# Reordering steps 19 to 50 and the casts beside 128-token tiles in a fused attention, MLP and expert kernel

## The chip, the cores and the metric

One core of a Trainium2 chip runs the whole kernel. The metric is device time in microseconds, the median of several runs; lower is better. TensorE's two clock levels are 1.2 and 2.4 GHz; the profile gives the granted share of the upper one.

## The reference, cut to what matters

Attention with keys and values averaged over groups of 8, then a dense ELU layer, then a top-1 mixture of 8 experts:

```python
k_p = k.reshape(B, H, Sp, 8, D).mean(axis=3)        # B=8, H=8, S=576, Sp=72, D=64
v_p = v.reshape(B, H, Sp, 8, D).mean(axis=3)
attn = softmax(q @ k_p.T / 8)                        # 576 x 72 per head
x = concat_heads(attn @ v_p)                         # 4608 tokens x 512
h = x @ w_in                                         # 512 -> 2048, w_in as float64
x = elu(h) @ w_out                                   # 2048 -> 512, w_out as float64
e = argmax(x @ w_gate); p = softmax(x @ w_gate)[e]   # 8 experts
out = p * (relu(x @ w1[e]) @ w2[e])                  # 512 -> 1024 -> 512
```

## The kernel before, in words

Work is put on the engines by hand: within a stretch, the order in which Python calls the helpers is the order of each engine's own queue.

**The dense layer** has 12 blocks of 384 tokens (3 tiles of 128) and 16 slices of the hidden width, so 192 steps. Step n does `g1_mm` (12 matmuls into one of two `h` banks of PSUM), the ELU, and `g2` of step n-2 (9 matmuls into the three `y` banks). An operand is split in a high and a low half (`xh`, `xl`; `gh`, `gl`). On ScalarE (ACT) a step has `elu_a` (three activations, lines 517 to 519) and the cast `gh` (line 531); on VectorE (DVE) `elu_b` (lines 524 and 525) and `gl` (line 532). Because there are two `h` banks, `h` of step n+2 waits until `elu_b` of step n has read its bank. When a block, or a quarter of blocks 0 and 1, ends, the three `y` banks are emptied (`y_rows`, lines 563 to 567, or `y_join`, line 589) before the next block's first `g2` may write them.

Other work is hung into named slots of a step through `at(n, slot, fn, ...)`; the order of the slots stands in `step`. Four kinds of it matter here.

- Steps 0 to 27 decode the float64 weights: `w_mul` (ACT, line 221), `w_bits` (DVE, lines 226 to 232), `w_hi` (ACT, line 243), `w_lo` (DVE, line 246). The later decode tiles, the parked partial sums that `y_fetch` brings back (SP queue, line 582) and nothing else by then share a ring of four buffers (tag `st`).
- Attention tiles 6 to 35: `s_mm` (32 small matmuls, line 411), `s_max` (DVE, line 418), `s_exp` (ACT, line 427, four heads a call), `s_norm` (DVE, lines 431 to 433). Up to tile 8, `t_mm` transposes on TensorE and `t_copy` empties the banks (line 471); from tile 9 on `q_turn` (DVE, line 447) and `q_move` (ACT and DVE by turns, line 455) do it in blocks. `pv_mm` (line 480) and `pv_copy` follow. Three banks (`bank_a`) serve `s_mm`, `t_mm` and `pv_mm`.
- Gate logits: `r_logit` (DVE, line 600), one for each expert and tile; `route_at` has a list of how many go into each step.
- `y_park` and `y_fetch` move partial sums of blocks 0 and 1 to memory and back.

**The experts** come as a list of tiles: D (512 tokens), S (256), T (128), U (32). `mix(n)` does a quarter n of them in turn: first matmuls `m_g1` (line 1249), second matmuls `m_g2` of the quarter before (line 1284), `m_act` (lines 1261 and 1262), `m_out` (lines 1301 and 1303), then the small U tile that runs beside it, then block moves of a later tile's rows (`m_move`, line 1155: 8 copies on ACT and 8 on DVE), then `ahead`. That is a planner: it loads weights (SP queue) and splits them into halves (`m_split`: casts on ACT, line 130, differences on DVE, line 131) up to a reach in estimated time and as far as slots of 4 KB are free. T tiles T0, T1 and T2 are quarters 28 to 31, 36 to 39 and 44 to 47; a T quarter has 16 first and 6 second matmuls. Tiles that are not "turned" by block moves (D0 to D3, T, U) are transposed on TensorE (line 1181), 88 transposes of 128x128 in all.

Of the kernel before, what the change touches and what calls it, by code (L numbers as in the profile page):

```python
# [10 lines left out]
F32 = mybir.dt.float32  # L11
# [87 lines left out]
def fused_kernel(ctx: ExitStack, tc: tile.TileContext, q, k, v, w_in, w_out, w_gate, w1, w2, cst, out):  # L99
# [459 lines left out]
    def y_rows(blk, plus=None):  # L559
        yr = mrpool.tile([P, TB, ROW], F32, tag="yr", name=f"yr{blk}")  # L560
        for j in range(TB):
            if plus:
                nc.vector.tensor_add(yr[:, j, :DM], plus[j], ys[blk][j])  # L563
            elif j % 2 == 0:
                nc.scalar.copy(yr[:, j, :DM], ys[blk][j])  # L565
            else:
                nc.vector.tensor_copy(yr[:, j, :DM], ys[blk][j])
        return yr
# [128 lines left out]

    SCORE0 = (6, 8)

    def score_at(t, n, slot="pe_mid"):  # L700
        at(n, slot, s_mm, t)
        n += slot == "pe_end"
        for hh in range(2):
            at(n, "dve_pre", s_max, t, hh)
        at(n, "act_mid", s_exp, t, 0)
        n += t not in (7, 8)
        at(n, "act_mid", s_exp, t, 1)
        at(n, "dve_mid" if t in SCORE0 else "end", s_norm, t)

    def turn_at(t, n):  # L710
        at(n + 1, "end", q_turn, t)
        for part in range(2):
            at(n + 2 + part, "act_mid", q_move, t, part)

    def trans_at(t, n):
        at(n, "pe_end" if t in OUT else "pe_mid", t_mm, t)
# [15 lines left out]
    for t in range(2 * TB, NT):  # L732
        if t not in SCORE:
            blk, j = divmod(t, TB)
            SCORE[t] = (NF * (blk - 1) + 5 * j - 2 if blk > 3 else 2 * NF - 1 + 5 * j, "pe_mid")
            if t > T_TURN:
                at(SCORE[t][0], "pe_mid", pv_mm, t - 1)
                at(SCORE[t][0], "act_mid", pv_copy, t - 1)
            at(SCORE[t][0] - 6, "end", a_load, t)
        else:  # L740
            at(SCORE[t][0] - 6, "end", a_load, t)
        score_at(t, *SCORE[t])
        if t >= T_TURN:
            turn_at(t, SCORE[t][0])
        else:
            trans_at(t, TRANS[t])
    at(NF * (NBLK - 1) - 2, "pe_mid", pv_mm, NT - 1)
# [53 lines left out]
    at(3 * QF + 1, "evac", y_park, 1, 1)  # L801
    at(5 * QF + 1, "evac", y_park, 0, 2, 0)
    for j in range(TB):
        at(4 * QF + 1 + j, "end", y_fetch, 0, j)
        at(6 * QF + 2 + j, "end", y_fetch, 1, j)
        at(7 * QF + 1 + j, "act_end", y_fetch, 2, j)

# [16 lines left out]
            at(n + 3, "pe_mid", r_count, blk)  # L824
            at(n + 3, "end", r_put, blk)

    route_at(1, 30, [1, 2, 2, 2, 2, 3, 3, 3, 3, 3])
    route_at(0, 41, [2, 2] + [3] * 6 + [2])
    route_at(2, 3 * NF + LAG + 1, [2, 2, 2, 2, 3, 3, 3, 3, 4])
    for blk in range(3, last):  # L830
        route_at(blk, NF * (blk + 1) + LAG, [3, 2, 3, 2, 3, 2, 3, 2, 2, 2])
# [306 lines left out]
    def m_turn(it, half):  # L1138
# [7 lines left out]
            nc.vector.transpose(t[:, x], g[:, x, :DM].rearrange("p (b f c) -> p b c f", b=4, c=KC))  # L1146
        spun[it, half] = t

    def m_move(it, half):
        name = f"{it[0]}{it[1]}_{half}"  # L1150
        t = spun.pop((it, half))
        w = moved[it, half] = w_tile([P, KC, 2, P], F32, f"zm{name}")
        for n, (a, b) in enumerate((a, b) for a in range(4) for b in range(4)):
            copy = (nc.vector.tensor_copy, nc.scalar.copy)[n % 2]
            copy(
                w[BL * b:BL * (b + 1), :, :, BL * a:BL * (a + 1)],
                t[BL * a:BL * (a + 1), :, b].rearrange("p x c t -> p c x t"),
            )
        w_free(f"zt{name}")

    def m_trans(it, u):
        kind, s = it
        if u == 0 and kind in "DS":
            zs[it, 0] = [pools[0].tile([P, KC, 2 * ST], F32R, tag=f"z{x}", bufs=1, name=f"z{x}{kind}{s}") for x in "hl"]
        if it in turned:
            half = {0: 0, turned[it]: 1}.get(u)
            if (it, half) in moved:
                src = moved.pop((it, half)).rearrange("p c x t -> p c (x t)")
                hi, lo = (z[:, :, 2 * P * half:2 * P * (half + 1)] for z in zs[it, 0])
                nc.scalar.copy(hi, src)  # L1170
                nc.vector.tensor_sub(lo, src, hi)
                w_free(f"zm{kind}{s}_{half}")
            return
        t = rows.pop((it, u))
        if u == 0:
            gates[it] = pools[0].tile([P, 4], F32, tag="gate", bufs=6, name=f"gate{kind}{s}")
        nc.vector.tensor_copy(gates[it][:, u:u + 1], t[:, DM:DM + 1])
        ps = bank_z([P, KC, P], f"zT{kind}{s}_{u}")
        t = t[:, :DM].rearrange("p (k c) -> p c k", c=KC)
        for c in range(KC):  # L1180
            nc.tensor.transpose(ps[:, c], t[:, c], ident)  # L1181
        if kind in "TU":
            z = mrpool.tile([P, KC, P], F32, tag="wgb1", name=f"zf{kind}{s}")
            nc.scalar.copy(z, ps)
            zs[it, 0] = z
            return
        hi, lo = (z[:, :, u * P:(u + 1) * P] for z in zs[it, 0])
        nc.scalar.copy(hi, ps)
        nc.vector.tensor_sub(lo, ps, hi)

    def m_load(it, i):
        kind, s = it
        regs, at = where[it]
        if i == 0:
            e = nc.sync.value_load(regs[0:1, 0, at:at + 1], min_val=0, max_val=NE - 1)
            wts[it] = [e]
        e = wts[it][0]
        if kind in "DS":
            st = staged(f"w1st{kind}{s}_{i}").rearrange("p (c f) -> p c f", c=KC)
        else:  # L1200
            st = w_tile([P, KC, 2 * P], F32, f"t1{kind}{s}_{i}")
        nc.sync.dma_start(
            st, w1[bass.ds(e, 1), :, 2 * P * i:2 * P * (i + 1)].rearrange("o (p c) f -> p (o c) f", p=P)
        )
        if kind == "U":
            st2 = w_tile([P, 2, DM], F32, f"t2{s}_{i}")
        else:
            st2 = staged(f"w2st{kind}{s}_{i}").rearrange("p (c d) -> p c d", c=2)
        nc.sync.dma_start(
            st2, w2[bass.ds(e, 1), 2 * P * i:2 * P * (i + 1), :].rearrange("o (c p) d -> p (o c) d", p=P)  # L1210
        )
        raws2[it, i] = st, st2
# [132 lines left out]
    def u_g2(it):  # L1345
# [4 lines left out]
        for n, (i, u) in enumerate(terms):  # L1350
            for j in range(4):
# [6 lines left out]
                    stop=n == len(terms) - 1,  # L1358
                )
        w_free(*(f"t{y}{k}{s}_{i}" for i in range(4) for y, k in (("1", "U"), ("2", ""))))  # L1360
        o = mrpool.tile([P, P], F32, tag="yr", name=f"uo{s}")
        nc.scalar.mul(o, ps, gates[it][:, 0:1])
        scatter(out.rearrange("n (j d) -> (n j) d", j=4), o, sidxs[it][0][:, 1:2], 4 * NTOK)
# [76 lines left out]
    for k in range(1, len(main)):  # L1440
        kind, prev = main[k][0], main[k - 1][0]
        for u in range(TILES[kind]):
# [4 lines left out]
            else:  # L1447
                n = 4 * k - 1
            (trans_late if prev != "T" and u > 1 else trans_at).setdefault(n, []).append((main[k], u))
    moves = {}  # L1450
    for k in range(TURN_FROM, len(main)):
        it, far = main[k], main[k - 1][0] == "T"
        if it[0] != "T":
            turned[it] = 1 + far
            n = 4 * k - 4 if far else 4 * k - 1
            if it[0] == "D":
                plan = ((3, m_turn, 0), (2, m_move, 0), (2, m_turn, 1), (1, m_move, 1))
# [40 lines left out]
    def mix(n):  # L1498
# [12 lines left out]
            m_out(main[k0], i0)  # L1511
        if k in side:
            (m_trans_side, u_g1, u_trans, u_g2)[i](side[k])
        for fn, it2, half in moves.pop(n, ()):
            fn(it2, half)
        ahead(n)
        for fn, *args in chores.pop(n, ()):
            fn(*args)
        if n == 13:
# [35 lines left out]
    def alone(it):  # L1555
# [9 lines left out]
        if it[0] == "U":  # L1565
            u_g1(it)
            u_trans(it)
            u_g2(it)
            return
        for i in range(4):  # L1570
            m_g1(it, i)
# [66 lines left out]
```

## Time and profile before

| | |
|---|---|
| median of 3 runs | 1367.85 us (1367.63 to 1370.15) |
| profiled execution | 1372.5 us, of which the span is 1370.4 us |
| TensorE busy | 98% of the span (weight loads 85%) |
| VectorE, ScalarE, GpSimd busy | 74%, 59%, 15% |
| mean granted clock | 0.994 |
| steps 0 to 191 of the dense layer | from 25.4 us to 918.9 us |

A row of the timeline gives start and length in us, engine, line, operation and tiles, and in brackets the idle time of the engine before it and what ended it. TensorE is nearly always busy, so the rows to look for are the few in which TensorE itself has such a bracket, and above them the row of the engine that is named there.

### The profile page before, as it was taken

How to read it: one execution, taken by the hardware profiler on the slowest of the kernel's cores; microseconds unless marked ns; L12 is line 12 of the kernel's file. 1: busy time of each engine (PE TensorE's matmuls, PEld its weight loads, DVE VectorE, ACT ScalarE, POOL GpSimd, SP SyncE). 2: the span in 40 equal slices, each digit the busy share in tenths (PEclk: the TensorE clock that was granted, in tenths of full speed). 3: DMA queues.
4: the chain of work that ended last, by engine and by line, in shares of the span. 5: the costliest groups of instructions: out<-in, count | busy, mean ns of one | idle time of the engine just before them, and what ended most of it. 6: DMA issues, size and time to landing. Idle time of an engine off the chain costs nothing.

```text
span 1370.4 us, 23752 instructions
## 1 busy us (share of the span) xinstructions
PE 1345.3 (98%) x8409; PEld 1159.5 (85%) x8410; DVE 1020.8 (74%) x2467; ACT 801.8 (59%) x1952; POOL 209.9 (15%) x208
## 2 busy tenths in 40 slices
PE   8999899999999999999999999999999999999998
PEld 5799788888888889898988888888888888787877
DVE  7898979988887879797878786886556765546361
ACT  6777766666766676666666665561333544545261
POOL 0011011101111211121210000120221142112030
PEclk9999999999999999999999999999999999999999
DMA  9157434637454463555451332564576357749360
GB/s 347 67 172 215 121 76 97 89 67 82 69 85 72 71 80 61 87 65 86 73 86 47 62 40 47 101 155 117 174 106 200 99 183 276 266 162 348 128 244 23
DMA packets 109145, 169.43 MB, mean 124 GB/s; under 512 B 15509, under 2 KB 53015, under 8 KB 109016
## 3 DMA queue, kind: packets, MB, share of 16 engines
q1 hardware_dynamic: 91528, 135.45, 39.2%
q0 software_dynamic: 17488, 32.37, 11.8%
q8 instruction: 68, 1.11, 0.4%
q14 instruction: 61, 0.50, 0.2%
HBM read 146.35 MB, written 21.88 MB: 123 GB/s over the span
## 4 chain that ended last, share of the span: by engine, by line
PE 83%; DVE 5%; issue 4%; ACT 4%; DMA 2%; POOL 1%; SPq 0%; POOLq 0%; DVEq 0%; ACTq 0%
PE h L507 26%; PE y L549 26%; PE mhD L1249 12%; PE myD L1284 12%; PE pv L480 3%; PE sp L411 2%; DVE dec L228 1%; DVE dec L232 1%; POOL out_dram L1307 1%; ACT gh L531 1%; PE vsum L346 1%; ACT dec L221 1%; DVE dec L226 1%; PE zTD L1181 1%; DMA wgb<-in_moe_w_gate_dram 0%
## 5 line engine op out<-in xcount | busy, mean ns | idle before, releaser
L549 PE MATMUL y<-woh,gh 128*128 128x512 f32 x576 | 230.5, 400 | 6.6 <-DVE yr L563 2.4
L549 PE MATMUL y<-wol,gh 128*128 128x512 f32 x576 | 226.7, 394 | 0.0
L549 PE MATMUL y<-woh,gl 128*128 128x512 f32 x576 | 226.6, 393 | 0.0
L600 DVE SCALAR_TENSOR_TENSOR junk<-yr,wgb 128x512 bf16<-128x512 f32 x264 | 180.9, 685 | 5.2 <-ACT yr L565 1.2
L531 ACT CAST gh<-g 128x384 fp32r<-128x384 f32 x192 | 98.6, 514 | 126.6 <-DVE g L525 107.2
L507 PE MATMUL h<-xh,wih 128*128 128x384 f32 x768 | 168.5, 341 | 1.5 <-ACT xh L493 1.5
L507 PE MATMUL h<-xl,wih 128*128 128x384 f32 x768 | 166.6, 338 | 0.0
L507 PE MATMUL h<-xh,wil 128*128 128x384 f32 x768 | 165.4, 336 | 0.0
L524 DVE SCALAR_TENSOR_TENSOR g<-g,th 128x384 f32<-128x384 f32 x192 | 106.4, 554 | 74.1 <-ACT th L519 73.8
L507 PEld LDWEIGHTS h<-xh,wih 128*128 128x128 f32 x768 | 139.3, 189 | 18.0 <-ACT xh L493 2.0
L517 ACT ACTIVATE th<-h 128x384 f32<-128x384 f32 x192 | 94.2, 490 | 97.4 <-PE h L507 96.7
L1261 ACT ACTIVATE hhD<-mhD 128x512 fp32r<-128x512 f32 x64 | 38.3, 599 | 182.5 <-PE myD L1284 175.3
L1262 DVE SCALAR_TENSOR_TENSOR hlD<-mhD,hhD 128x512 fp32r<-128x512 f32 x64 | 44.2, 691 | 132.5 <-ACT hhD L1261 132.5
L507 PEld LDWEIGHTS h<-xl,wih 128*128 128x128 f32 x768 | 137.7, 189 | 0.2
L507 PEld LDWEIGHTS h<-xh,wil 128*128 128x128 f32 x768 | 137.3, 188 | 0.0
L549 PEld LDWEIGHTS y<-woh,gh 128*128 128x128 f32 x576 | 108.1, 188 | 28.5 <-issue 2.9
L549 PEld LDWEIGHTS y<-woh,gl 128*128 128x128 f32 x576 | 108.3, 188 | 23.8
L532 DVE TENSOR_TENSOR gl<-g,gh 128x384 fp32r<-128x384 f32 x192 | 106.9, 557 | 23.4 <-ACT gh L531 18.7
L549 PEld LDWEIGHTS y<-wol,gh 128*128 128x128 f32 x576 | 108.3, 188 | 16.3
L525 DVE TENSOR_TENSOR g<-g,h 128x384 f32<-128x384 f32 x192 | 106.3, 554 | 6.6
L519 ACT ACTIVATE th<-th 128x384 f32<-128x384 f32 x192 | 100.9, 525 | 6.1
L518 ACT ACTIVATE g<-th 128x384 f32<-128x384 f32 x192 | 100.8, 525 | 6.1
(289 smaller groups left out, 2402.6 us busy)
## 6 DMA issues: line engine op xcount, KB each, us to landing
wgb<-in_moe_w_gate_dram SPq DMA_DIRECT2D x96, 256.0 KB
w1stD<-in_moe_w_dram SPq DMA_DIRECT2D x32, 512.0 KB
w2stD<-in_moe_w_dram SPq DMA_DIRECT2D x32, 512.0 KB
qT<-in_q_dram SPq DMA_DIRECT2D x36, 256.0 KB
ybuf<-yr SPq DMA_DIRECT2D x33, 256.5 KB
raw<-in_moe_w_in_dram SPq DMA_DIRECT2D x16, 512.0 KB
raw<-in_moe_w_out_dram SPq DMA_DIRECT2D x15, 512.0 KB
t1U<-in_moe_w_dram SPq DMA_DIRECT2D x12, 512.0 KB
```

The source lines that it names most:

```text
L507: mark["g1"] = nc.tensor.matmul(ps, wi[i][a][:, c, o:o + P], bb[blk][:, c, :], start=n == 0, stop=n == 3 * KC - 1).ins
L517: nc.scalar.activation(th, hps[blk, f], AF.Relu, scale=-1.0)
L518: nc.scalar.activation(g, th, AF.Exp, scale=-1.0)
L519: nc.scalar.activation(th, th, AF.Tanh, scale=-0.5)
L524: nc.vector.scalar_tensor_tensor(g, g, 1.0, th, op0=ALU.add, op1=ALU.mult)
L525: nc.vector.tensor_max(g, g, hps.pop((blk, f)))
L531: nc.scalar.copy(gh, g)
L532: nc.vector.tensor_sub(gl, g, gh)
L549: nc.tensor.matmul(ys[blk][j], a[:, js], wo[i][bb][:, o, :], start=n == 0 and f in FIRST[blk], stop=n == 2 and f in LAST[blk],)
L600: nc.vector.scalar_tensor_tensor(junk, yrows[blk][j][:, :DM], 1.0, pes[blk, e], op0=ALU.mult, op1=ALU.mult, accum_out=lgs[blk][:, j, e:e + 1])
L1249: mark["g1"] = nc.tensor.matmul(ps[:, x], a[:, c, o * P:(o + 1) * P], y[:, c], start=k == 0, stop=k == len(terms) - 1).ins
L1284: nc.tensor.matmul(yps[it][u], a[:, us], second[w][:, o], start=i == 0 and o == 0 and n == 0, stop=i == 3 and o == 1 and n == 2,)
```

## The change

`y_rows`: of the three copies that empty the `y` banks, the first two go to ScalarE and the third to VectorE (first and third, and second). `score_at`: tile 7's score matmuls go behind `g2`, its maxima into `dve_mid`, and some exponentials of tiles 6, 7 and 8 into `act_end`, behind the cast `gh`; tile 8's `s_norm` goes to the step's end. `turn_at`: for tile 9 everything is one step later; for tiles 12, 15, ... 33 the second part of the moves goes into `act_end`. One `y_fetch` is a step later. The lists of logits for blocks 1 and 0 are dealt out anew, over the same steps. In `mix`, where the tile before a D or S tile is a T tile (quarters 27 and 35), `ahead` comes in front of the block moves, whose target slot is taken first; and U's last multiply and scatter (`u_out`) are a function of their own, behind the moves in those two quarters. Tiles that are not turned read each transpose's 128 columns side by side instead of every fourth, with the rows of `w1` loaded in the matching order.

```diff
             if plus:
                 nc.vector.tensor_add(yr[:, j, :DM], plus[j], ys[blk][j])
-            elif j % 2 == 0:
+            elif j < 2:
                 nc.scalar.copy(yr[:, j, :DM], ys[blk][j])
...
-    def score_at(t, n, slot="pe_mid"):
-        at(n, slot, s_mm, t)
-        n += slot == "pe_end"
+    def score_at(t, n):
+        at(n, "pe_end" if t == 7 else "pe_mid", s_mm, t)
         for hh in range(2):
-            at(n, "dve_pre", s_max, t, hh)
-        at(n, "act_mid", s_exp, t, 0)
+            at(n, "dve_mid" if t == 7 else "dve_pre", s_max, t, hh)
+        at(n, "act_end" if t in (6, 7) else "act_mid", s_exp, t, 0)
         n += t not in (7, 8)
-        at(n, "act_mid", s_exp, t, 1)
-        at(n, "dve_mid" if t in SCORE0 else "end", s_norm, t)
+        at(n, "act_end" if t in (7, 8) else "act_mid", s_exp, t, 1)
+        at(n, "dve_mid" if t == 6 else "end", s_norm, t)
...
-            at(n + 2 + part, "act_mid", q_move, t, part)
+            at(n + 2 + part, "act_end" if part and t > T_TURN and t % TB == 0 else "act_mid", q_move, t, part)
...
-            turn_at(t, SCORE[t][0])
+            turn_at(t, SCORE[t][0] + (t == T_TURN))
...
-        at(4 * QF + 1 + j, "end", y_fetch, 0, j)
+        at(4 * QF + 1 + j + (j == 2), "end", y_fetch, 0, j)
...
-    route_at(1, 30, [1, 2, 2, 2, 2, 3, 3, 3, 3, 3])
-    route_at(0, 41, [2, 2] + [3] * 6 + [2])
+    route_at(1, 30, [2, 3, 3, 1, 1, 2, 3, 3, 3, 3])
+    route_at(0, 41, [2] + [3] * 6 + [2, 2])
...
-        t = t[:, :DM].rearrange("p (k c) -> p c k", c=KC)
         for c in range(KC):
-            nc.tensor.transpose(ps[:, c], t[:, c], ident)
+            nc.tensor.transpose(ps[:, c], t[:, c * P:(c + 1) * P], ident)
...
-            st, w1[bass.ds(e, 1), :, 2 * P * i:2 * P * (i + 1)].rearrange("o (p c) f -> p (o c) f", p=P)
+            st,
+            w1[bass.ds(e, 1), :, 2 * P * i:2 * P * (i + 1)].rearrange(
+                "o (p c) f -> p (o c) f" if it in turned else "o (c p) f -> p (o c) f", p=P
+            ),
...
             turned[it] = 1 + far
+            if far:
+                casts_first.add(4 * k - 5)
...
-        for fn, it2, half in moves.pop(n, ()):
+        todo_now = moves.pop(n, ())
+        if n in casts_first:
+            for _, it2, half in todo_now:
+                m_room(it2, half)
+            ahead(n)
+        elif k in side and i == 3:
+            u_out(side[k])
+        for fn, it2, half in todo_now:
             fn(it2, half)
-        ahead(n)
+        if n not in casts_first:
+            ahead(n)
+        elif k in side:
+            u_out(side[k])
```

`m_room` takes the slot that `m_move` writes; `u_out` holds the last three lines of the old `u_g2` (multiply by the gate on ACT, scatter on GpSimd's queue).

## Rows read from the trace of the kernel before

**Rows 1.** The page's first part: busy time, share of span, instructions by engine

```profile
PE 1345.3 (98%) x8409; PEld 1159.5 (85%) x8410; DVE 1020.8 (74%) x2467; ACT 801.8 (59%) x1952; POOL 209.9 (15%) x208
```

**Rows 2.** Timeline of steps 20 to 22: start, length, engine, line, [idle, releaser]

```profile
133.10 0.66 ACT L221 ACTIVATE dec<-raw 128x512 f32<-128x512 f32 x1 [1.77 <-DVE wil L246]
...
135.41 0.56 DVE L532 TENSOR_TENSOR gl<-g,gh 128x384 fp32r<-128x384 f32 x1 [2.34 <-ACT gh L531]
...
139.43 1.88 DVE L563 TENSOR_TENSOR yr<-part,y 128x512 f32<-128x512 f32 x3
...
140.26 0.47 PE L549 MATMUL y<-woh,gh 128*128 128x512 f32 x1 [2.41 <-DVE yr L563]
```

**Rows 3.** Timeline of steps 24 to 27

```profile
151.22 0.72 PE L411 MATMUL sp<-kT,qT 64*64 64x72 f32 x30 [1.30 <-ACT aT L471]
...
161.11 0.56 DVE L525 TENSOR_TENSOR g<-g,h 128x384 f32<-128x384 f32 x1
...
163.00 0.96 PE L507 MATMUL h<-xh,wih 128*128 128x384 f32 x4
```

**Rows 4.** Timeline of steps 33 and 34

```profile
200.18 1.02 DVE L455 COPY aT<-turned 32x256 f32<-32x256 f32 x3
...
201.23 1.88 DVE L589 TENSOR_TENSOR part<-part,y 128x512 f32<-128x512 f32 x3
...
202.07 0.47 PE L549 MATMUL y<-woh,gh 128*128 128x512 f32 x1 [1.51 <-DVE part L589]
```

**Rows 5.** Timeline of steps 49 and 50

```profile
274.57 1.23 ACT L455 COPY aT<-turned 32x256 f32<-32x256 f32 x3
...
276.38 0.56 DVE L525 TENSOR_TENSOR g<-g,h 128x384 f32<-128x384 f32 x1
276.46 0.50 PE L549 MATMUL y<-woh,gh 128*128 128x512 f32 x1 [1.45 <-ACT yr L565]
...
277.88 0.69 DVE L567 COPY yr<-y 128x512 f32<-128x512 f32 x1
...
278.63 0.51 PE L549 MATMUL y<-woh,gh 128*128 128x512 f32 x1 [1.21 <-DVE yr L567]
```

**Rows 6.** Windows: stretch, length, busy by engine, clock, DMA share, GB/s

```profile
238.00:276.00 38.00, 37.01 (x227) 32.96 (x225) 36.73 (x109) 25.71 (x76) 6.34 (x6) 1.00 0.57 82
279.00:283.00 4.00, 4.00 (x14) 3.58 (x13) 3.20 (x12) 0.63 (x2) 0.00 (x0) 0.57 0.43 164
1306.00:1312.00 6.00, 6.00 (x32) 5.03 (x31) 2.63 (x5) 5.90 (x11) 0.64 (x1) 1.00 0.02 3
1320.00:1324.00 4.00, 3.09 (x11) 2.70 (x12) 4.00 (x5) 2.37 (x4) 3.69 (x2) 0.57 1.05 398
```

**Rows 7.** Timeline of quarters 27 to 30 (around tile T0)

```profile
1241.06 3.31 ACT L1155 COPY zmD<-ztD 32x256 f32<-32x256 f32 x8
...
1245.48 2.36 DVE L131 TENSOR_TENSOR m2lT<-w2stT,m2hT 128x1024 fp32r<-128x1024 f32 x2 [3.36 <-ACT m2hT L130]
...
1250.14 0.50 PE L1284 MATMUL myT<-m2hT,hhT 128*128 128x512 f32 x1 [0.26 <-ACT oD L1301]
...
1251.71 0.50 PE L1284 MATMUL myT<-m2hT,hlT 128*128 128x512 f32 x1 [0.83 <-DVE hlT L1262]
...
1255.63 0.50 PE L1284 MATMUL myT<-m2hT,hlT 128*128 128x512 f32 x1 [0.49 <-DVE hlT L1262]
```

**Rows 8.** Timeline of quarter 38 (tile T1)

```profile
1318.30 0.51 PE L1284 MATMUL myT<-m2hT,hhT 128*128 128x512 f32 x1 [0.59 <-ACT hhT L1261]
...
1320.91 0.80 PE L1284 MATMUL myT<-m2hT,hlT 128*128 128x512 f32 x1 [1.89 <-DVE hlT L1262]
```

**Rows 9.** Weight loads of lines 1181 and 1249: duration in ns min/median/max

```profile
L1181 PEld LDWEIGHTS zTD<-ident,xgD x64: 196/209/220, 895.6 to 1051.9; 128*128 128x128 f32 x64
...
L1249 PEld LDWEIGHTS mhT<-zfT,t1T x192: 186/192/333, 1240.5 to 1360.6; 128*128 128x128 f32 x192
```

**Rows 10.** The chain in order of time, one piece: start, us, what

```profile
270.67 6.22 DMA wgb<-in_moe_w_gate_dram
```

More of the change, by code (lines that the diff above doesn't have):

```diff
@@ L741, in fused_kernel @@
             at(SCORE[t][0] - 6, "end", a_load, t)
-        score_at(t, *SCORE[t])
+        score_at(t, SCORE[t][0])
         if t >= T_TURN:
-            turn_at(t, SCORE[t][0])
+            turn_at(t, SCORE[t][0] + (t == T_TURN))
         else:
@@ L1147, in m_turn, with m_room @@
         spun[it, half] = t
+    def m_room(it, half):
+        moved[it, half] = w_tile([P, KC, 2, P], F32, f"zm{it[0]}{it[1]}_{half}")
     def m_move(it, half):
@@ L1151, in m_move @@
         t = spun.pop((it, half))
-        w = moved[it, half] = w_tile([P, KC, 2, P], F32, f"zm{name}")
+        if (it, half) not in moved:
+            m_room(it, half)
+        w = moved[it, half]
         for n, (a, b) in enumerate((a, b) for a in range(4) for b in range(4)):
@@ L1360, in u_g2, with u_out @@
         w_free(*(f"t{y}{k}{s}_{i}" for i in range(4) for y, k in (("1", "U"), ("2", ""))))
+        acts[it, 2] = ps
+    def u_out(it):
+        s = it[1]
+        ps = acts.pop((it, 2))
         o = mrpool.tile([P, P], F32, tag="yr", name=f"uo{s}")
@@ L1449, in fused_kernel @@
             (trans_late if prev != "T" and u > 1 else trans_at).setdefault(n, []).append((main[k], u))
-    moves = {}
+    moves, casts_first = {}, set()
     for k in range(TURN_FROM, len(main)):
@@ L1568, in alone @@
             u_g2(it)
+            u_out(it)
             return
```

## Prediction

> **What bounds the kernel now.** I read the page first: TensorE is busy 98% of the span [rows 1], so only time in which TensorE waits or runs at the lower clock can be won. The list of its instructions in order of time then shows where that is: apart from the first five steps and the very end, TensorE stands still at few places, and they are the places that the diff touches. The timeline around each says who is late.
>
> Step 22 waits 2.41 us for the first of three additions that empty a `y` bank [rows 2]. VectorE (DVE) is late there because it stood idle 2.34 us for the cast `gh` of step 20, which lay on ScalarE (ACT) behind four exponentials and behind a decode multiply that had itself waited 1.77 us for a buffer that DVE had still to free [rows 2]. Step 24 waits 1.30 us for the copy out of a transpose bank [rows 3], step 34 1.51 us for `y_join`, which lies behind 1.02 us of block moves on DVE [rows 4]. Step 50 waits 1.45 us for an ACT copy that lies behind 1.23 us of moves, and 1.21 us for a DVE copy that lies behind `elu_b` and more moves [rows 5]; right after that the granted clock is at 1.2 GHz for part of 279 to 283 (mean 0.57) [rows 6]. At T0 the second matmuls wait 0.26, 0.83 and 0.49 us [rows 7], at T1 0.59 and 1.89 us [rows 8], again with a stretch at the lower clock [rows 6].
>
> The idle just listed is 2.41+1.30+1.51+2.66+1.58+2.48 = 11.9 us. Each stretch at the lower clock is about 3.4 us: a mean of 0.57 over 4 us needs 0.86 x 4 at half. It costs half of that, 1.7 us, so 3.4 us for both. That is the pot, 15.3 us or 1.1%.
>
> **The change part by part.**
>
> *Steps 20 to 22.* With `y_fetch` of part 2 a step later, three of the ring's four buffers are taken in step 20 instead of four, so the multiply needs no wait; with the exponentials behind `gh`, the cast follows `elu_b` at once. DVE's 2.34 us go, but ACT's next `elu_a` still comes behind the four exponentials, which keeps back some 0.5: the additions move up from 139.43 by about 1.9. The wait falls from 2.41 to about 0.5: -1.9. The late fetch is one DMA on SP's queue, read by the third addition; its price is a rival below.
>
> *Step 24.* The score matmuls go behind nine `g2` matmuls (some 2.1 us of cover), and the copy that they wait for ends before that: 1.30 becomes about 0.1, -1.2. Maxima and eight exponentials are now behind `gh`, so `gl` is no later; but `elu_a` of step 25 and `s_norm` are behind the exponentials, and `s_norm` on DVE holds up step 25's decode. So `elu_b` of step 25, now over at 161.11+0.56 = 161.67 [rows 3], comes only about 1.3 us earlier, at 160.35: of its lead of 1.9 DVE loses some 0.6 to exponentials that run to the end of eight times 0.3 us. `h` of step 27, now at 163.00 [rows 3], needs that bank. TensorE, 3.1 us ahead by the two waits won and some 0.4 more by their starts (below), would come at 159.5 and must wait: +0.9. This is the next thing late.
>
> *Steps 28 to 31.* Exponentials and `s_norm` of tile 8 behind `gh`: DVE and ACT have idle time here once decoding is over, so 0.
>
> *Steps 32 to 36.* Tile 9's turn leaves step 32 and its moves leave step 33; one logit more stands in step 32. `y_join` comes up by about 1.3 (1.02 of it the three DVE moves): 1.51 becomes about 0.1, -1.4. The moves now end in step 35 just when step 36 wants them for `pv_mm`: +0.3. Logits and their weight loads on SP move by at most one step inside steps 30 to 35; every `wgb` load is issued at the same step or one earlier.
>
> *Steps 41 to 50.* DVE is busy 36.73 of 38 us [rows 6], so a logit pulled from step 48 to 42 only moves work within a full queue: 0, and at most 0.3 at two banks. In step 49 the ACT copies lose 1.23 us of moves ahead of them: the wait of 1.45 becomes about 0.25. Bank 1 is then emptied by ACT too, and DVE's only copy, bank 2, comes straight behind `elu_b` (over at 276.94 [rows 5]): 277.65. TensorE wants it at 276.6: about 1.05 in place of 1.21. Together 2.66 becomes 1.3: -1.4. Standing still for half as long, TensorE should keep the upper clock: -1.7.
>
> *Later joins.* The same order at blocks 3 to 10, where waits are at most 0.3 us: -0.3 in all. Moves behind `gh` delay the next `elu_a` by 1.23, which ACT's idle time covers; were it gone, `elu_a` would be late by that and `h` two steps on would show it.
>
> *T0, quarter 27.* By counting slots the planner loads and splits the same units, but for one load of U2 that goes a quarter later. Now ACT waits for the U multiply and then moves for 3.31 us before the casts, and DVE waits 3.36 us for them [rows 7]. With casts first both start about 5 us sooner. The same work now starts without hanging on the U matmuls, so the moves, at the end, finish about 1.4 us earlier than the casts did, and all that quarter 28 queues behind (`zh`, `hhT`, `oD`, then `hlT`) is earlier. The waits of 1.58 become about 0.3: -1.3. The U scatter, later on GpSimd's queue, writes output that nobody reads.
>
> *T1, quarter 35.* Casts first likewise, and the S tile's loads, whose staging slots these casts free, start some 5 us sooner, in a stretch where the DMA share is 0.02 [rows 6]. But quarter 36 still splits two S units between `hhT` and `hhT`: I get 1.0 and 0.75 left of 2.48, so -0.7. With the longest stop halved, the lower clock goes: -1.7.
>
> *Transposes.* 88 weight loads, now of every fourth column, show a median of 209 ns against 192 ns for T's first matmuls, which read side by side [rows 9]; matmul starts differ less, about 3 ns, so I take -0.3; the ends are 0 and 17 ns x 88 = 1.5 us. "SBUF — State Buffer" of the Trainium skill (the note on cachelines) says that successive reads of one 16-byte line run at full bandwidth and each new line costs; four fp32 apart is a new line every time. By that rule the whole 1.5 us would come back and the sum would be 1.2 us lower; the 17 ns agree in sign with it.
>
> *Sum.* -1.9 -1.2 +0.9 -1.4 +0.3 -1.4 -1.7 -0.3 -1.3 -0.7 -1.7 -0.3 = -10.7. Starts of matmuls show a little more lost at a wait than its recorded idle (278.63 minus 276.46 is 2.17 [rows 5] for three matmuls of about 0.23: 1.48 lost, 1.21 recorded); 0.2 at each of eight waits makes -1.6, so -12.3. That stands against the profiled execution: 1372.5 us, its span 1370.4 and 2.1 around it, 4.65 above the median of 1367.85. What makes it longer is not shown, and the stretches at the lower clock may be part of it, so I count half of their 3.4 us in the timed runs: -10.6, **1357.3 us**. With all of it: 1355.6; with none: 1359.0.
>
> **The rivals.**
>
> *A: VectorE stays the bound in steps 19 to 50.* Its queue is nearly full there [rows 6], and what TensorE wins at steps 22, 24 and 50 comes back as waits of `h` for `elu_b`. For it: the 0.9 us that I already find at step 27. Against: 2.34 us of DVE idle really goes. It takes 1.9+1.2-0.9+1.4 and 0.8 of the supplement: 1361.7 us.
>
> *B: casts first only moves the wait at T0 and T1.* DVE's eight copies (2.4 us) now stand between the casts and `hlT`. For it: two S units remain in front of `hhT`. It takes 1.3+0.7, the supplement of 0.6 and the half clock of 0.85: 1360.8 us.
>
> *C: the change does not do what it says.* The waits have other ends: a buffer of the ring that is not free after all, copies that another queue holds. A, B and step 34 fail together: 1357.3+4.4+3.5+1.6 = 1366.8 us, no change within 0.2%, which is about what a measurement of this kernel can tell from none.
>
> *D: slower, by the late fetch.* The third addition of step 21 needs part 2 at about 138.9, and its load is issued at about 133.1 instead of 128.7. A transfer of the same 256 KB took 6.22 us on the chain [rows 10], which would cost 0.4. Every us later costs one, as DVE stands with all of step 22 behind it; the sign turns when it lands after 138.9+10.6 = 149.5, 16 us after issue. [...] Against it: SP issues nothing else between 133 and 141.
>
> **How the numbers follow.** Forecast 0.64, A 0.14, B 0.10, C 0.07, D 0.05. Faster by over 0.2%: 0.64+0.14+0.10 = 0.88; within: 0.07; slower: 0.05. The low end: all waits that I left (0.5+0.1+0.9+0.1+0.3+1.3+0.3+1.75 = 5.25) gone: 1352.0. The high end lies beyond A and B at 1363.0, which leaves out C, D and a mixture of A with B.
>
> **What would show it right or wrong.** Right: no idle of DVE for `gh` in step 20; a wait of about 0.5 at step 22; a new one of about 1 us at `h` of step 27, released by line 525; at step 50 one wait for the DVE copy; the clock at 1.00 in both stretches; `m2lT` without its 3.36 us. Wrong: those DVE idles still there, TensorE waits at other joins, ACT late with `elu_a` behind exponentials or moves, or the U matmuls late for their load.

## The result and the profile after

The changed kernel takes 1356.53 us (median of 6 runs, 1355.2 to 1358.9) against 1368.21 us for the kernel before (6 runs beside it, 1367.46 to 1370.15): 11.7 us less, ratio 0.9913 with a 95% interval of 0.9900 to 0.9926. That is faster, as forecast, by about one microsecond more than the 1357.3 us predicted. The two profiled executions differ by more, 1372.5 to 1355.2 us: the profiled execution of before was longer than any of the six timed beside, and 1.7 of the 17.3 us lie in step 0, which the change does not touch (first `h` matmul of step 0 to that of step 1: 8.4 us before, 6.8 after; the stretch at the lower clock near 30 us was 6.8 us long before and 3.4 after).

The first part of the page, to be held against [rows 1]:

```profile
PE 1337.6 (99%) x8410; PEld 1152.3 (85%) x8410; DVE 1019.0 (75%) x2467; ACT 800.8 (59%) x1952; POOL 205.5 (15%) x208
```

The timeline of steps 20 to 22 of the changed kernel, against [rows 2]:

```profile
129.83 0.67 ACT L221 ACTIVATE dec<-raw 128x512 f32<-128x512 f32 x1
...
131.14 0.52 ACT L531 CAST gh<-g 128x384 fp32r<-128x384 f32 x1 [0.64 <-DVE g L525]
131.69 0.56 DVE L532 TENSOR_TENSOR gl<-g,gh 128x384 fp32r<-128x384 f32 x1
...
136.07 1.87 DVE L563 TENSOR_TENSOR yr<-part,y 128x512 f32<-128x512 f32 x3
...
136.90 0.47 PE L549 MATMUL y<-woh,gh 128*128 128x512 f32 x1 [0.66 <-DVE yr L563]
```

The multiply has no bracket any more, `gl` follows without its idle of 2.34 us, and the wait of TensorE is 0.66 in place of 2.41. Steps 24 to 27, against [rows 3]:

```profile
148.25 0.73 PE L411 MATMUL sp<-kT,qT 64*64 64x72 f32 x32
...
154.47 0.17 DVE L431 TENSOR_SCALAR sm<-sm 128x8 f32<-128x8 f32 x1 [1.77 <-ACT s L427]
...
157.96 0.55 DVE L525 TENSOR_TENSOR g<-g,h 128x384 f32<-128x384 f32 x1
...
158.56 0.97 PE L507 MATMUL h<-xh,wih 128*128 128x384 f32 x4 [0.51 <-DVE g L525]
```

The score matmuls of tile 7 no longer wait. What is late next is `elu_b` of step 25, held up by `s_norm`, which itself waits 1.77 us for eight exponentials; `h` of step 27 waits 0.51 us for it. In step 34 TensorE has no bracket [rows 4]. Step 50, against [rows 5]:

```profile
269.30 1.06 ACT L565 COPY yr<-y 128x512 f32<-128x512 f32 x2
...
269.92 0.50 PE L549 MATMUL y<-woh,gh 128*128 128x512 f32 x1 [0.22 <-ACT yr L565]
...
270.50 0.55 DVE L525 TENSOR_TENSOR g<-g,h 128x384 f32<-128x384 f32 x1
270.97 0.68 DVE L567 COPY yr<-y 128x512 f32<-128x512 f32 x1
```

2.66 us of waits have become 0.36 (0.22 here, 0.14 at 271.71 for the DVE copy). Two more waits are new, both of `h` for `elu_b`, in steps 46 and 62:

```profile
248.61 0.96 PE L507 MATMUL h<-xh,wih 128*128 128x384 f32 x4 [0.28 <-DVE g L525]
...
322.72 0.44 PE L507 MATMUL h<-xh,wih 128*128 128x384 f32 x1 [0.41 <-DVE g L525]
```

At T0 ACT casts first, then moves, then multiplies for U; the differences on DVE (`m2lT`) wait 0.24 us in place of 3.36, and no second matmul of T0 waits [rows 7]:

```profile
1227.94 1.98 ACT L130 CAST m2hT<-w2stT 128x1024 fp32r<-128x1024 f32 x2
...
1229.01 2.36 DVE L131 TENSOR_TENSOR m2lT<-w2stT,m2hT 128x1024 fp32r<-128x1024 f32 x2 [0.24 <-ACT m2hT L130]
...
1231.84 3.31 ACT L1159 COPY zmD<-ztD 32x256 f32<-32x256 f32 x8
...
1235.18 0.37 ACT L1373 ACTIVATE uo<-uy,gateU 128x128 f32<-128x128 f32 x1
```

At T1 two waits are left, behind the S units that quarter 36 still splits in front of `hlT` [rows 8]:

```profile
1303.25 1.22 DVE L131 TENSOR_TENSOR m2lS<-w2stS,m2hS 128x1024 fp32r<-128x1024 f32 x1
...
1304.39 0.42 DVE L1268 SCALAR_TENSOR_TENSOR hlT<-mhT,hhT 128x256 fp32r<-128x256 f32 x1
...
1304.86 0.50 PE L1290 MATMUL myT<-m2hT,hlT 128*128 128x512 f32 x1 [0.61 <-DVE hlT L1268]
...
1308.59 0.50 PE L1290 MATMUL myT<-m2hT,hlT 128*128 128x512 f32 x1 [0.30 <-DVE hlT L1268]
```

Windows right behind the joins of step 50 and of T1 (columns as in [rows 6]: the granted clock comes after the busy times) now show 1.00:

```profile
272.00:276.00 4.00, 4.00 (x47) 3.44 (x50) 3.86 (x13) 2.43 (x6) 0.00 (x0) 1.00 0.07 9
...
1303.00:1310.00 7.00, 6.10 (x40) 4.90 (x39) 6.64 (x9) 4.37 (x6) 2.17 (x2) 1.00 1.04 369
```

In all, TensorE's recorded waits of over 0.1 us behind the first five steps fall from 12.09 us in eleven places to 3.12 us in eight.

### The profile page after: what moved, and what is told of

Read it like the earlier page. It is cut to its first block, busy times and chain, and to the rows that moved or that the text cites. A ratio compares the mean times of both kernels' runs of the same rounds, so it can differ in the third digit from the quotient of the medians.

```text
span 1353.3 us, 23757 instructions
## 1 busy us (share of the span) xinstructions
PE 1337.6 (99%) x8410; PEld 1152.3 (85%) x8410; DVE 1019.0 (75%) x2467; ACT 800.8 (59%) x1952; POOL 205.5 (15%) x208
```

## The experiments

Two measures are used beside the timed ratios, because many effects here are smaller than the intervals (about 0.15%, 2 us). One is the list of TensorE's waits. The other is the length of a stretch, from the first `h` matmul of one step to that of another, or from the first matmul of T0 or T1 to the first matmul of the tile behind it. A number in brackets behind a length is the time at the lower clock in it.

| kernel | steps 19-24 | 24-29 | 49-54 | T0 | T1 |
|---|---|---|---|---|---|
| before | 25.00 | 26.12 | 27.65 (3.4) | 19.30 | 21.72 (3.4) |
| p1_steps | 22.99 | 25.08 | 23.99 | 19.31 | 22.03 |
| p2_experts | 26.45 (3.4) | 24.55 | 28.79 (6.8) | 16.93 | 18.36 |
| p3_side | 26.17 (3.4) | 24.60 | 28.75 (6.8) | 19.30 | 21.96 (3.4) |
| p4_uout | 24.90 | 26.14 | 28.07 (3.4) | 17.40 | 20.51 |
| p5_casts | 26.43 (3.4) | 24.58 | 26.21 | 18.46 | 20.14 |
| changed kernel | 23.27 | 25.06 | 23.95 | 16.92 | 18.35 |
| after2 (the same) | 23.39 | 25.06 | 23.92 | 16.92 | 18.35 |
| u1_fetch | 24.26 | 25.12 | 23.87 | 16.93 | 18.36 |
| u3_exps6 | 23.28 | 25.13 | 24.11 | 16.93 | 18.37 |
| u2_rows | 23.08 | 25.12 | 25.82 | 17.53 | 18.37 |
| u4_s7 | 22.98 | 26.20 | 23.97 | 16.92 | 18.36 |
| b1_all | 23.53 | 25.87 | 24.71 | 16.92 | 16.92 |
| b2_cap | 22.97 | 25.07 | 23.96 | 16.92 | 16.92 |

A length carries a spread of its own. Steps 19 to 24 are the same code in p1_steps, the changed kernel, after2, u2_rows, u4_s7 and b2_cap and take 22.97 to 23.39 us; T0 is the same code in u2_rows and the changed kernel and takes 17.53 and 16.92 (u2_rows has a wait there behind 2.46 us of idle of ACT for which the profile names no cause on this core).

### The three parts, each alone on the kernel before

**p1_steps**: of the diff, only `y_rows`, `score_at`, `turn_at`, `y_fetch` and the two lists of `route_at`.

> Only the part in steps 19 to 50 (y_rows, score_at, turn_at, y_fetch, both logit lists). Theory by the sum of the prediction: -1.9 -1.2 +0.9 -1.4 +0.3 -1.4 -0.3 = -5.0 us of waits, -1.0 for five of the eight waits, and between 0 and -1.7 for the stretch at the lower clock after step 50: 6.0 to 7.7 us below the kernel before, ratio 0.9944 to 0.9956. From the step lengths of the changed kernel (-1.46 us of a clock difference in step 0 left out) I now expect the upper end, about -8.0 us by the profile, less what of the clock stretch is in the profiled execution alone. Rival A (VectorE gives the wins back as waits of h for elu_b): at most -3.5 us, and waits on line 525 in the list of TensorE's waits that add up to over 2 us.

Measured: 1361.95 us, ratio 0.9938 (0.9923 to 0.9953), 8.5 us by the ratio: the upper end of what was expected and a little more. Waits of `h` on line 525 add up to 1.02 us, so rival A does not hold for the change as a whole.

**p2_experts**: of the diff, only `m_room`, `u_out` and `casts_first`.

> Only casts in front of the moves and U's last multiply and scatter behind them, in quarters 27 and 35. Theory by the sum of the prediction: -1.3 -0.7 -0.6 and between 0 and -1.7 for the clock after T1: 2.6 to 4.3 us below the kernel before, ratio 0.9969 to 0.9981; the trace of the changed kernel shows -2.4 at T0 and -3.4 at T1 and so speaks for some 5.0 (0.9963). Rival B (the wait only moves to another join): within 1.0 us of the kernel before, with waits of over 2 us left in quarters 28 to 30 and 36 to 38.

Measured: 1364.94 us, ratio 0.9957 (0.9942 to 0.9972), 5.9 us, more than the 2.6 to 4.3 of the prediction's sum and the 5.0 read from the trace. Nothing waits at T0, 0.92 us at T1. Rival B (the wait only moves) is ruled out.

**p3_side**: of the diff, only the transposes and the rows of `w1`.

> Only the transposes that read their 128 columns side by side, and the rows of w1 in the matching order. The prediction took -0.3 us, with ends of 0 and -1.5. The changed kernel shows weight loads of 140 ns in place of 209 ns and 10 ns less for each of 88 matmuls: by the loads 69 ns x 88 = 6.1 us if they were on the path, by the starts of matmuls about -0.9 us. Expected -0.9 us (ratio 0.9993); a rival by which every weight load is exposed gives -6 us (0.9956).

Measured: 1370.48 us, ratio 0.9998 (0.9984 to 1.0011): no difference that the timing can tell, and not the 6 us that exposed loads would give. The profile shows the small one. In every kernel with the new transposes the steps 186 to 190, which hold the 16 of D0, take 18.35 in place of 18.6, and the stretches from one D tile's first matmul to the next one's, with 16 each, 44.27 in place of 44.37 and twice 45.69 in place of 45.85: some 0.27 + 0.10 + 2 x 0.16 = 0.7 us for 64 of the 88. (The profiled run of p3_side itself was one of its longest, 1373.8 us, and has a single wait of 1.72 us at 1032.40 that no other kernel shows; I have no cause for it.) The rows of the transposes, before and changed (shortest, median, longest in ns):

```profile
L1181 PE MATMUL zTD<-ident,xgD x64: 270/283/308, 895.8 to 1052.1; 128*128 128x128 f32 x64
```

```profile
L1184 PEld LDWEIGHTS zTD<-ident,xgD x64: 138/140/143, 885.2 to 1040.9; 128*128 128x128 f32 x64
L1184 PE MATMUL zTD<-ident,xgD x64: 271/273/327, 885.4 to 1041.0; 128*128 128x128 f32 x64
```

The weight load went from 209 [rows 9] to 140 ns, the matmul by 10 ns, and it is the 10 ns that the path shows.

The three ratios together give -0.62 - 0.43 - 0.02 = -1.07%, the whole change -0.87% in one measurement and -0.98% in another (after2 below); with intervals of 0.13 to 0.15% on each, the parts add up.

### T0 and T1: the casts or U's multiply?

The part has two edits. **p4_uout** makes one of them on the kernel before, **p5_casts** the other:

```diff
# p4_uout, quarters 27 and 35
+        if n not in casts_first and k in side and i == 3:
+            u_out(side[k])
         for fn, it2, half in todo_now:
             fn(it2, half)
         ahead(n)
+        if n in casts_first and k in side:
+            u_out(side[k])
# p5_casts, quarters 27 and 35
+        if k in side and i == 3:
+            u_out(side[k])
+        if n in casts_first:
+            for _, it2, half in todo_now:
+                m_room(it2, half)
+            ahead(n)
         for fn, it2, half in todo_now:
             fn(it2, half)
-        ahead(n)
+        if n not in casts_first:
+            ahead(n)
```

> On the kernel before, only U's last multiply and scatter are moved behind the block moves and the planner's casts of quarters 27 and 35; the casts stay behind the moves. If it is the wait of ScalarE for U's matmuls that made the casts late, most of the win comes without the casts going first: 2 to 4 us below the kernel before, and m2lT's idle of 3.36 us shrinks by what ScalarE had waited for the multiply. If it is the 3.31 us of moves in front of the casts, next to nothing is won (under 1 us) and the idle of m2lT stays at about 3 us.

> On the kernel before, the planner's casts of quarters 27 and 35 go in front of the moves, but U's last multiply and scatter stay in front of both. With p4_uout (-1.9 us of step time at T0, -1.2 at T1) and p2_experts (-2.4 and -3.4, 1.7 of it the clock) this closes the square. If casts and U's multiply are two waits in a row on ScalarE, each taken away by itself gives part: T0 -1.0 to -1.9, T1 -1.5 to -3.4, in all 2.5 to 5 us below the kernel before. If U's multiply is the one that holds, this gives under 1 us and m2lT still waits over 1.5 us.

Measured: p4_uout 1366.46 us, ratio 0.9975 (0.9963 to 0.9987); p5_casts 1367.41 us, ratio 0.9973 (0.9962 to 0.9984). Either edit alone is worth 3.4 to 3.7 us, both 5.9. In the stretches: T0 19.30 with neither, 18.46 with casts first, 17.40 with U behind, 16.93 with both. At T0 U's multiply is thus the larger part, the first of the two cases expected of p4_uout; p5_casts has the sign expected of its second case (`m2lT` waits over 1.5 us) but wins 3.7 us, more of it at T1 (1.6 to 1.9 us in the stretches) than at T0 (0.84). The rows of p4_uout and then of p5_casts at T0 say why:

```profile
1241.33 2.36 DVE L131 TENSOR_TENSOR m2lT<-w2stT,m2hT 128x1024 fp32r<-128x1024 f32 x2 [1.43 <-ACT m2hT L130]
```

```profile
1237.95 0.37 ACT L1372 ACTIVATE uo<-uy,gateU 128x128 f32<-128x128 f32 x1 [1.54 <-PE uy L1358]
...
1239.28 2.36 DVE L131 TENSOR_TENSOR m2lT<-w2stT,m2hT 128x1024 fp32r<-128x1024 f32 x2 [2.15 <-ACT m2hT L130]
```

With U's multiply in front, ACT stands 1.54 us for U's matmuls whatever comes behind; with it at the back, `m2lT` waits 1.43 us in place of 3.36, though the moves still precede the casts. At T1 the lengths are 20.51 with U behind, 20.14 with casts first, 18.36 with both, against 21.72 to 22.03 with neither. Which edit is the larger there is not shown: p4_uout has in it, at 1314.76, a TensorE wait of 0.55 us behind 1.25 us of idle of ACT for which the profile names no cause. The loads count too. In p1_steps, whose casts are late, ACT waits four times for weights of the S and T tiles; the longest of these waits, and TensorE's wait for the `hhT` that stands behind it on ACT:

```profile
1307.46 1.04 ACT L130 CAST m2hS<-w2stS 128x1024 fp32r<-128x1024 f32 x1 [1.14 <-DMA w2stS<-in_moe_w_dram]
1308.84 0.50 PE L1283 MATMUL myT<-m2hT,hhT 128*128 128x512 f32 x1 [1.60 <-ACT hhT L1260]
```

The kernel before (0.81 and 0.57 us), p3_side (1.38 and 0.59) and p4_uout (1.55 and 0.77) have such waits for loads at T1 too; the ten profiles with casts first have none. The S tile's second four loads are issued 6.2 to 8.5 us behind T1's first matmul in the kernel before, 2.7 to 5.3 in p5_casts and 0.8 to 3.5 in the changed kernel. So the casts that go first free the staging slots early enough for these loads.

### Step 22: the fetch or the exponentials?

**u1_fetch** and **u3_exps6** take one edit each out of the changed kernel:

```diff
# u1_fetch
-        at(4 * QF + 1 + j + (j == 2), "end", y_fetch, 0, j)
+        at(4 * QF + 1 + j, "end", y_fetch, 0, j)
# u3_exps6
-        at(n, "act_end" if t in (6, 7) else "act_mid", s_exp, t, 0)
+        at(n, "act_end" if t == 7 else "act_mid", s_exp, t, 0)
```

> The changed kernel with y_fetch of part 2 back at the end of step 19. Theory of the prediction (four ring buffers taken in step 20, the decode multiply in front of the cast gh waits for DVE's wil): the multiply of step 20 starts behind wil at about 131.65 in place of 129.83, gh about 1.2 us later than 131.14, DVE idle for it about 1.8 in place of 0.64, and the wait at step 22 grows from 0.66 to 1.6 to 2.2 us: +1.0 to +1.5 us, ratio 0.992 to 0.993. Rival (the exponentials alone held gh back, the fetch has no part): no idle in front of the multiply of step 20, step 22 as in the changed kernel, no difference.

> The changed kernel with the first four exponentials of tile 6 back in front of gh in step 20 (0.3 us each), the fetch still late. Theory: gh comes 1.2 us later, DVE idle for gh 1.8 in place of 0.64; elu_a of step 21 is then no later than now (the same work in front of it), so the additions of step 21 move by at most what DVE loses, and step 22 waits 0.7 to 1.9: 0 to +1.2 us. Rival: the order of gh and the exponentials is worth the larger part of the 1.75 us that step 22 won: +1.2 us or more.

Measured: u1_fetch 1359.02 us, ratio 0.9910 (0.9895 to 0.9926); u3_exps6 1356.99 us, ratio 0.9900 (0.9884 to 0.9916). The times cannot tell them apart, the rows can. u1_fetch:

```profile
133.32 0.66 ACT L221 ACTIVATE dec<-raw 128x512 f32<-128x512 f32 x1 [1.77 <-DMA raw<-in_moe_w_out_dram]
...
134.42 0.56 DVE L532 TENSOR_TENSOR gl<-g,gh 128x384 fp32r<-128x384 f32 x1 [1.13 <-ACT gh L531]
...
139.64 0.47 PE L549 MATMUL y<-woh,gh 128*128 128x512 f32 x1 [1.67 <-DVE yr L563]
```

u3_exps6:

```profile
131.77 0.56 DVE L532 TENSOR_TENSOR gl<-g,gh 128x384 fp32r<-128x384 f32 x1 [0.48 <-ACT gh L531]
...
136.52 0.47 PE L549 MATMUL y<-woh,gh 128*128 128x512 f32 x1 [0.67 <-DVE yr L563]
```

With the early fetch the multiply waits 1.77 us again, as in [rows 2]. The row names a load, but `wil` of that step ends at 133.29, 0.03 us before the multiply starts: a wait for two things is put down to one of them. Steps 19 to 24 take 25.00 before, 24.26 with only the exponentials moved, 23.28 with only the fetch moved, 23.27 with both. Within the spread of 0.4 us the fetch is the whole win; the exponentials win only where the fetch is early.

### Steps 24 and 50 undone

**u4_s7** puts the score matmuls of tile 7 back in front of `g2`, **u2_rows** the copies and the second parts of the moves where they were:

```diff
# u4_s7
-        at(n, "pe_end" if t == 7 else "pe_mid", s_mm, t)
+        at(n, "pe_mid", s_mm, t)
# u2_rows
-            elif j < 2:
+            elif j % 2 == 0:
-            at(n + 2 + part, "act_end" if part and t > T_TURN and t % TB == 0 else "act_mid", q_move, t, part)
+            at(n + 2 + part, "act_mid", q_move, t, part)
```

> The changed kernel with the score matmuls of tile 7 back in front of the nine g2 matmuls of step 24; maxima and exponentials stay late. Theory: the wait of 1.30 us for the copies of aTp comes back there, and the wait of 0.51 us for elu_b at h of step 27 shrinks or goes, since TensorE comes that much later: 0.5 to 1.3 us above the changed kernel. Rival A (TensorE is held by VectorE here in any case, so that the 1.30 us were only moved): within 0.3 us of the changed kernel, h of step 27 starting where it does now against step 22.

> The changed kernel with the copies of the y banks dealt out as before (first and third on ACT, second on DVE) and every second part of the moves back in front of gh. Theory: in step 50 the two waits of 1.45 and 1.21 us are back in place of 0.22 and 0.14, and the granted clock falls to 1.2 GHz right behind them for 3.4 us or twice that, as in all four profiles so far that have these waits: +2.3 to +2.8 us of waits and +1.7 to +3.4 of clock in the profile, ratio 0.993 to 0.996. Rival (the clock falls there for a reason of its own, or because TensorE had other stops before): the waits are back, the clock stays at 1.00 in the profile, +2.5 us. If the granted clock falls without the waits being back, the theory of the clock is wrong.

Measured: u4_s7 1355.76 us, ratio 0.9910 (0.9896 to 0.9924), which the timing does not separate from after2 beside it. Its profile does:

```profile
147.13 0.72 PE L411 MATMUL sp<-kT,qT 64*64 64x72 f32 x30 [1.41 <-ACT aT L471]
```

The wait is back, the one at `h` of step 27 is gone, and steps 24 to 29 take 26.20 in place of 25.06: 1.14 us, so rival A fails here. u2_rows: 1359.62 us, ratio 0.9910 (0.9894 to 0.9925). Its two waits in step 50:

```profile
272.54 0.50 PE L549 MATMUL y<-woh,gh 128*128 128x512 f32 x1 [1.62 <-ACT yr L565]
...
273.96 0.50 PE L549 MATMUL y<-woh,gh 128*128 128x512 f32 x1 [0.45 <-DVE yr L567]
```

and the window behind them:

```profile
272.00:281.00 9.00, 8.01 (x76) 6.50 (x77) 7.33 (x21) 6.31 (x19) 0.00 (x0) 1.00 0.19 50
```

The waits are back (25.82 against 23.95 for steps 49 to 54, +1.9 us), the lower clock is not: my theory of the clock fell, the rival held (with 1.9 us in place of its 2.5). u2_rows takes out two edits together, the copies and the moves, and no run tells which of them wins. p5_casts then showed the same, with the waits of before (1.53 and 1.20) and a clock of 1.00. The stretch follows such waits in some executions, in others not (below).

u2_rows shows one thing more. Steps 112 to 176, four blocks far behind the changed lists, take 288.15 us in all eight profiles that have the new `y_rows` and moves, and 290.05 in u2_rows, 288.63 to 289.81 in the five without them: 0.5 to 1.9 us, although hardly a wait is recorded there.

### The control, and two kernels that go further

**after2** is the changed kernel once more. **b1_all** makes five more moves, one for each wait left:

```diff
-            at(n, "dve_mid" if t == 7 else "dve_pre", s_max, t, hh)
+            at(n, "dve_mid" if t in (6, 7) else "dve_pre", s_max, t, hh)
-        at(n, "dve_mid" if t == 6 else "end", s_norm, t)
+        at(n + (t == 7), "dve_mid" if t in (6, 7) else "end", s_norm, t)
-    SCORE = {6: (20, "pe_mid"), 7: (24, "pe_mid"), 8: (28, "pe_mid")}
+    SCORE = {6: (21, "pe_mid"), 7: (24, "pe_mid"), 8: (28, "pe_mid")}
-    route_at(0, 41, [2] + [3] * 6 + [2, 2])
+    route_at(0, 41, [2, 3, 2, 3, 3, 3, 3, 3, 2])
-    route_at(2, 3 * NF + LAG + 1, [2, 2, 2, 2, 3, 3, 3, 3, 4])
+    route_at(2, 3 * NF + LAG + 1, [2, 2, 2] + [3] * 6)
...
+        cap = main[seq[n][0]][0] == "T"
-                if what == "split" and (need, it, i) not in units[:todo["load"]]:
+                if what == "split" and ((need, it, i) not in units[:todo["load"]] or cap == 2):
...
                     m_split(it, i)
+                    cap *= 2
```

**b2_cap** has only the last two of the five, the list of block 2 and the cap of one split in a quarter of a T tile.

> The changed kernel once more, as the measure of the other runs on this chip: ratio 0.990 to 0.9926, the same eight waits of 3.1 us in all, and, if the clock falls only where TensorE has stood still for over a microsecond, no stretch at 1.2 GHz but the one near 30 us (3.4 or 6.9 us long, both seen) and the end.

> The changed kernel with five more moves, one for each wait that its trace still shows: tile 6's scores a step later and its maxima behind the additions (0.66 us at step 22), s_norm of tile 7 a step later (0.51 at h of step 27), one logit of block 0 from step 43 to 47 (0.28 at h of step 46), one of block 2 from step 59 to 54 (0.41 at h of step 62), and at most one weight split in a quarter of a T tile (0.61 and 0.30 at T1). Theory (TensorE's waits are the only thing left, each gone without a new one): 2.8 us of recorded waits and 0.2 us more at each of six, so 2.8 to 4.0 us below the changed kernel, ratio 0.9885 to 0.9893. Rival (VectorE is full in these steps, so each wait turns up at the next bank): less than 1 us below the changed kernel, and new waits on line 525 or 563 of together over 1.5 us.

> The changed kernel with only two of the five moves of b1_all: at most one weight split in a quarter of a T tile, and one logit of block 2 from step 59 to 54; tile 6, tile 7 and block 0 stay as in the changed kernel. Theory: T1 (from its first quarter to the first S matmul) takes 16.9 us as in b1_all in place of 18.35, h of step 62 does not wait, and the waits that b1_all made at 143.50, 158.99 and 273.15 (0.85, 1.13 and 0.87 us) are not there: 1.4 to 2.0 us below the changed kernel, ratio 0.9875 to 0.9895, recorded waits of 1.8 us in all. Rival: the split units put off at T1 come back as a wait for weights in the S tile (over 0.5 us behind its first matmul), and the time is that of the changed kernel within 0.5 us.

Measured: after2 1355.26 us, ratio 0.9902 (0.9889 to 0.9916), seven waits of 2.93 us in all; step 62 does not wait this time, so the 0.41 us there is not a fixed cost of the change. b1_all: 1355.70 us, ratio 0.9903 (0.9890 to 0.9917), no faster than after2. T1 won 1.43 us (16.92 in place of 18.35), and steps 22, 27, 46 and 62 no longer wait, but new waits took their place. The three largest, the first two with the end of `s_norm` above them:

```profile
142.60 0.76 DVE L433 TENSOR_TENSOR s<-s,sm 128x576 f32<-128x576 f32 x1
...
143.50 0.73 PE L463 MATMUL aTp<-ident,s 64*72 64x64 f32 x16 [0.85 <-ACT g L518]
...
158.08 0.76 DVE L433 TENSOR_TENSOR s<-s,sm 128x576 f32<-128x576 f32 x1
...
158.99 0.73 PE L463 MATMUL aTp<-ident,s 64*72 64x64 f32 x16 [1.13 <-DVE s L433]
...
273.15 0.50 PE L549 MATMUL y<-woh,gh 128*128 128x512 f32 x1 [0.87 <-DVE yr L567]
```

A fourth, of 0.40 us, is at 1255.10 in the D tile behind T0. The time came out as the rival said, its waits did not: it named lines 525 and 563. The first two are transposes left where they were, behind a softmax that b1_all put a step later: `s_norm` of tile 6 ends at 143.36, that of tile 7 at 158.84. Only the third, the copy of bank 2, is a win that comes back at the next bank. b2_cap: 1353.96 us, ratio 0.9885 (0.9865 to 0.9905), waits of 1.86 us in all, T1 at 16.92 and no wait for weights behind it, all as expected. It is the shortest of all, but its interval overlaps that of the changed kernel; what is shown is the 1.43 us at T1 in its profile.

## Why the prediction was right, and where its sizes were off

The direction, the places and most of the named next waits came out as forecast; that the total came out so close is in part luck. Term by term, in the two profiled executions (where the prediction added 0.2 us a wait, this is included):

| term | predicted | measured | by |
|---|---|---|---|
| step 22 | -2.1 | -1.6 to -2.0 | steps 19-24, the six profiles with the same code |
| steps 24 and 27 | -0.5 | -1.1 | steps 24-29 |
| steps 34 and 36 | -1.3 | -1.4 | steps 33-37, 20.34 to 18.94 |
| logit pulled to step 42 | 0 | +0.5 | steps 44-49, 22.75 to 23.21 |
| step 50, waits | -1.8 | -1.9 to -2.3 | u2_rows, p5_casts against the changed kernel |
| step 50, clock | -1.7 | -1.4 to -1.8 | 27.65 against the same two |
| later joins | -0.3 | -0.5 to -1.9 | steps 112-176 |
| T0, and T1 with its clock | -4.3 | -2.4 - 3.4 = -5.8 | T0, T1 |
| transposes | -0.3 | -0.7 for 64 of 88 | steps 186-190, D tiles |

**Step 22.** Right in size, the reason half wrong. "With the exponentials behind `gh`, the cast follows `elu_b` at once" is true and wins nothing: u3_exps6 has the same 0.67 us. The late fetch is the cause. Rival D is ruled out: the additions run back to back in 1.87 us, so the third did not wait for its part, issued at 131.68.

**Steps 24 and 27.** The next thing late was named rightly, its size was 0.51 us in place of 0.9; and the wait won was larger than recorded, since step 24 shortened by 1.75 us for a recorded idle of 1.30. The Trainium skill, "Perfetto Trace Analysis" (Per-engine timelines), says that the end of a TensorE instruction in a profile is estimated and not observed; the rows are in line with it, and a wait is better sized by the starts of matmuls.

**Step 50.** The term that failed is the one that was costed at nothing, "a logit pulled from step 48 to 42 only moves work within a full queue: 0". It gave something at one end and took something at the other. In step 50 `elu_b` is over 1.35 us after bank 0 was wanted (271.05 against 269.92 - 0.22) in place of 1.93 (276.94 against 276.46 - 1.45), so the DVE copy made TensorE wait 0.14 us where I had 1.05. At step 46, behind the extra logit, `h` waits 0.28. b1_all, whose list puts a logit back from step 43 to 48 (not 47, as its expectation says), shows both again: no wait at step 46, 0.87 at bank 2.

**The clock.** I charged 1.7 us for each of two stretches and counted half of it in the timed runs. Across the profiles the stretch follows the waits, but not always: after step 22's wait of 1.9 to 2.4 us in three of five profiles (not in the kernel before), after step 50's in four of six, at T1 in two of five; after the single waits of 1.24 to 1.51 us at steps 24 (three profiles) and 34 (five) in none. The five profiles in which none of these waits is left (the changed kernel, after2, u3_exps6, b1_all, b2_cap) have no stretch but those at the beginning and the end. And its price depends on what comes next. Behind step 50 it costs what it seems: steps 49 to 54 take 25.82 and 26.21 us without it, 27.65 and 28.07 with 3.4 us of it, 28.75 and 28.79 with 6.8. Behind step 22 it costs 1.2 to 1.6 us at once and gives them back at step 24, whose wait of 1.30 is then gone: steps 19 to 29 sum to 51.12 and 51.04 us without it and to 51.00, 50.77 and 51.01 with it. At T1 the two profiles with the stretch (21.72, 21.96) are no longer than p1_steps without it (22.03). So the -1.7 at T1 is not shown as a term of its own, though p1_steps is the only profile to compare with and has more waits for loads there. The windows, p2_experts behind step 22 and step 50, then p5_casts behind step 50:

```profile
138.00:146.00 8.00, 6.40 (x24) 5.64 (x25) 7.65 (x16) 5.42 (x17) 1.67 (x2) 0.79 0.54 138
276.00:285.00 9.00, 7.80 (x35) 6.48 (x36) 5.86 (x17) 3.33 (x9) 0.00 (x0) 0.62 0.24 89
```

```profile
276.00:285.00 9.00, 7.80 (x77) 6.31 (x76) 7.34 (x21) 5.57 (x19) 0.00 (x0) 1.00 0.25 91
```

What the prediction left open, why the profiled execution was longer than the median, goes with these stretches. Of the kernel before, 53 timed runs are on record with their mean granted clock: the ten at 0.997 or more have a median of 1367.5 us, the 24 at 0.994 or less one of 1371.6. The profiled execution stood at 0.994; eleven runs of the changed kernel stand at 0.996 to 0.998.

**T0 and T1.** Both terms were too small. At T0 all three waits went, not all but 0.3 us; the sentence that carried it, that the work "now starts without hanging on the U matmuls", was the larger half. At T1 I had 1.0 and 0.75 us left and 0.61 and 0.30 remained; the early loads of the S tile, which I described but put no number on, are part of it.

**Later joins.** -0.3 was taken from recorded idle alone; by the starts, 288.15 us against a mean of 289.4 in the five kernels without the new order, it is four times that.

**Transposes.** The Trainium skill, "SBUF — State Buffer" (note on cachelines), says that reads which stay in one 16-byte line run at full bandwidth and each new line costs. The loads agree and by more than my upper end: I took 17 ns from T's first matmuls, it was 69 ns. The yardstick was wrong: T's own loads still take 192 ns in the changed kernel. But all but some 6 to 17 ns of the 69 were hidden.

**The rivals.** A fails for the whole (p1_steps, u4_s7); of its kind are only the small waits of `h` at steps 27, 46 and 62 and, in b1_all, the 0.87 us at bank 2. B fails (p2_experts). C fails with them, D by the additions of step 21.

**The total.** In the two profiled executions the measured terms add up to some 15.5 us where the sum had 12.3: T0, T1, the later joins and step 24 won more. From the profile to the timed runs I took off 1.7 us; it was 3.8, from 15.5 to the 11.7 measured. Two sizes that were too small thus offset each other, and the hit within about one microsecond is luck to that extent.

## What to carry to other kernels

On an engine without slack no move is free: cost it at the step that it leaves and at the step that it enters, each against the next deadline there, as the one logit between steps 42 and 48 shows. Where an edit takes two things out of a queue, try each alone before saying which one wins. And size waits by the starts of instructions over the whole stretch: recorded idle misses part of them, and a stretch at the lower clock may only take the place of the next wait.

## What the runs showed of the hardware that was not expected

The granted clock falls to 1.2 GHz behind the same wait in one execution and not in another (step 50: four profiles of six), in lengths of about 3.4 or 6.8 us; near 30 us one or the other length appears in every profile, and step 0 takes 6.8 us with the shorter and 7.2 to 8.4 with the longer. A weight load of 128 fp32 columns took 209 ns with every fourth column and 140 ns side by side, while the path became only 6 to 17 ns shorter for each transpose.
